# Moving one of two second-level minima to GpSimd, and the softmax statistics to one number per row, in a two-stage attention kernel

## The chip, the cores and the metric

The kernel runs on one core of one Trainium2 chip. The metric is the device time of one execution in microseconds (us); before the change the median of three runs is 1190.12 us (1189.49 to 1190.14). The engines are called by the profile's names: PE (TensorE), DVE (VectorE), ACT (ScalarE), POOL (GpSimd) and SP (SyncE, which issues the DMAs).

## The reference

Two attentions in a row, for 8 batches of 576 rows, float32:

```python
# 1: top-32 attention, 8 heads of width 64
scores = scale * np.matmul(q, k.transpose(0, 1, 3, 2))
kth = np.partition(scores, -32, axis=-1)[..., -32:-31]
scores = np.where(scores >= kth, scores, -1e9)
attn = softmax(scores)
x = np.matmul(attn, v)              # heads joined: 576 x 512 per batch
# 2: four experts (w_gate, wq, wk, wv, wo); the two with the larger logit count per row
logits = x @ w_gate
for e in range(4):
    a = softmax(causal(scale * (x @ wq[e]) @ (x @ wk[e]).T))
    out += weight_of(e) * (a @ (x @ wv[e]) @ wo[e])
```

## The kernel before, in words

**Tiling.** Two heads make a pair; there are 32 pairs, four to a batch. The 2 x 576 rows of a pair are nine tiles of 128 rows, in three groups of three tiles, so there are 96 groups in all. After every four pairs stands the second attention of that batch.

**One group (function `topk`).** PE multiplies the three tiles' scores, ACT copies them to `s` (L569). DVE then finds the 32 largest of each row of 576. It first folds the row: `f1` (L580) takes the larger of the halves into `fa`, `f3` (L583) the smaller into `fb`. `f4` folds `fa` once more: maxima of its halves into `cand` (L588), minima in place (L589), then from the maxima those of the next fold into `oct` (L591) and the minima beside them (L592). From there DVE works with MAX8 (eight largest of a row) and MATCH_REPLACE8 (strike eight values out): `f6` takes eight candidates from `fb` (L600), `f5` eight from each half of the minima in `fa` (L604, L605), and four rounds `win`/`rep` (L613, L618) take 8 of the 32 winners each, two from `oct` and two from `cand`.

POOL does small things for a group: `mark` (L596) copies one number of `oct` and so keeps what is queued behind it on POOL from starting earlier; `tails` (L608) copies the last candidates, and `compare` (L640), with a sign count on ACT, checks for the group before whether the candidates were enough. If the counts of the whole run say that they were not, a branch at L1249 runs a second, general pass over everything.

**Statistics (function `stats`, twice a pair).** For four or five tiles: differences to the row's maximum (`s1`, DVE, L700), exponentials (`s3`, ACT, L711), their sum (`s4`, DVE, L715), and logarithms. Maximum and logarithm go, each as a high and a low part, into four columns (`s2` on POOL, L706 and L707; `s6` on ACT, L725 and L726; `s7` on DVE, L730). PE transposes the four columns (`s8`, L734), ACT copies the rows into rows 64 to 67 of an operand (`s9`, L738), where the second product of the scores subtracts them.

**What sets the order.** Every step is a task with an engine, an assumed duration, a priority and buffers. `Plan.order` runs through them once with a table of priorities (`BIAS` and the `D_` numbers) and writes each engine's list of instructions; on the chip every engine follows its list in order. The list `PORT` names the DVE steps which the planner keeps apart from POOL's.

Of the kernel before, what the change touches and what calls it, by code (L numbers as in the profile page):

```python
# [10 lines left out]
FT = mybir.dt.float32  # L11
FR = mybir.dt.float32r
# [5 lines left out]
S = 576  # L18
D = 64
# [90 lines left out]
class Plan:  # L110
# [7 lines left out]
    PORT = ("f1", "f3", "f4", "s1", "s7", "ot", "constants", "sub", "low_again")  # L118
    SLACK = 100.9508
# [128 lines left out]
def pool(n):  # L248
# [7 lines left out]
BIAS = {"<lambda>": 432.2674, "again": 348.8874, "av": 0.3356, "avm": 369.6519, "c1": 80.5249, "c2": -8.8455, "c3":  # L256
        -45.1992, "c4": 1.7827, "c5": -12.4639, "cast": 189.9301, "cast_swap": 110.1952, "check1": 92.3392,
        "check2": 35.5895, "check3": -40.5142, "compare": -4.4354, "constants": -65.862, "copy": -161.6975, "count":
        229.2168, "diag": 42.7475, "dup": -188.6936, "dup1": -274.8919, "dup2": 295.4185, "e_stage": -264.9382,
# [3 lines left out]
        "g8": 176.5188, "g9": 85.871, "load_": -423.7509, "load_swap": -59.609, "loadv": 180.8196, "low_again":  # L263
        -141.4595, "m_stage": -469.5208, "mark": -298.151, "mask": 246.2406, "neg": 44.6072, "neg2": -127.4992,
# [3 lines left out]
        462.5432, "sub": 64.4327, "t_stage": 0.5767, "tails": 22.1925, "vproj": -19.8822, "win": 41.2933, "xh":  # L268
        154.0901, "xl": -80.96}
D_K2 = 84.27756  # L270
D_PREP = 21.53669
D_SC = 6.67649
D_TIE = -56.65601
D_MASK = -141.78759
D_STAT = -135.15358
D_TAIL = 0.07265
D_STEP = 0.10387
D_MOE = 4.215
D_LAST = 43.62471
D_PEN = 3.08857  # L280
D_SPAN = 3.51429
# [5 lines left out]
def kernel(ctx, tc, qk, vL, wq, wk, wv, wo, out):  # L287
# [42 lines left out]
    OCT = ring("oct", [P, 3, 72], FT, 2)  # L330
# [4 lines left out]
    STAT = sets("stat", 2, ([P, 5, TOPK], FT), ([P, 2, 5], FT), ([P, 5, 4], FR))  # L335
# [18 lines left out]
    def blank2(eng, x):  # L354
        t = K2[x].tiles[0]
        eng.memset(ft(t[0:64, gap(x)]), 0.0)
        eng.memset(ft(t[64:128, :]), 0.0)
        eng.memset(ft(t[64:68, OFF[x]:OFF[x] + S]), -8.0)
        eng.memset(ft(t[64:66, OFF[x]:OFF[x] + S]), -1.0)
# [11 lines left out]
    identf = sb.tile([P, P], FT, name="identf")  # L371
    identb = sb.tile([P, P], BF, name="identb")
# [177 lines left out]
    def topk(w, general):  # L550
# [4 lines left out]
        for g in range(3):  # L555
            js = (3 * g, 3 * g + 1, 3 * g + 2)
            s3, fa, fb, c = Buf(S3), Buf(FA), Buf(FB), Buf(CAND)
            oc = None if general else Buf(OCT)
# [26 lines left out]
            def f4(fa=fa, c=c, oc=oc):  # L585
# [37 lines left out]
            t = add("DVE", 1870, f4, [t], bufs=[fa, c, oc], prio=P0)  # L623
# [61 lines left out]
    def stats(w, x):  # L685
# [618 lines left out]
```

## Time and profile before

| what | before |
|---|---|
| median of 3 runs | 1190.12 us |
| the profiled execution's own time | 1187.17 us |
| its span, first to last instruction | 1185.4 us |
| busy PE / DVE / ACT / POOL | 1100.7 / 1090.6 / 982.9 / 377.2 us |
| granted TensorE clock, mean | 0.977 of full speed |

The profile is of one execution. Its span is the time between its first and last instruction; the execution's own time is 1.8 us longer. Busy time is time in which an instruction of the engine is recorded as running; instructions of one engine overlap a little, and starts are the safer measure: the time from the start of one instruction to that of the next is called a step here.

### The profile page before, as it was taken

Reading aid. Unit: us, or ns where it says so; the run is one execution under the profiler, and the core shown is the slowest. Engines: PE = TensorE matmul, PEld = TensorE weight load, DVE = VectorE, ACT = ScalarE, POOL = GpSimd, SP = SyncE. Lnnn points to the kernel's source line nnn. Section 1 sums busy time; section 2 is a strip of 40 time slices with the busy share of each in tenths; the row PEclk is TensorE's granted clock in tenths of the full one; section 3 lists DMA queues with packets and bytes.
Section 4 is the critical chain, followed back from the end, with each engine's and each line's share of the span. In section 5 each row is a group of like instructions: output and inputs, shape, how many; then the busy total and the mean of one; then the engine's idle time right before and its main releaser. Section 6 shows DMA issues by size and latency. Waiting matters only on the chain. (4 is left out here: it accounts for less than half of the span.)

```text
span 1185.4 us, 28265 instructions
## 1 busy us (share of the span) xinstructions
PE 1100.7 (93%) x9330; PEld 914.8 (77%) x9330; DVE 1090.6 (92%) x4745; ACT 982.9 (83%) x2050; POOL 377.2 (32%) x803
## 2 busy tenths in 40 slices
PE   3487799999999999999999999999999999999996
PEld 2366577787888878888888888888887878888785
DVE  7999999999999999999999999999999999999021
ACT  5677777989889997999889998899879997899554
POOL 4322222334323332243323333323332342322212
PEclk8689999999999999999999999999999999999999
DMA  7133332223432233333422233323432334320101
GB/s 204 44 92 87 83 91 64 77 63 100 123 92 68 72 105 84 82 91 94 116 82 69 64 99 111 92 67 93 118 82 61 83 101 118 93 51 21 39 6 44
DMA packets 45579, 98.56 MB, mean 83 GB/s; under 512 B 7792, under 2 KB 7792, under 8 KB 45424
## 3 DMA queue, kind: packets, MB, share of 16 engines
q1 hardware_dynamic: 45424, 96.67, 30.1%
q8 instruction: 76, 1.25, 0.4%
q14 instruction: 79, 0.65, 0.2%
HBM read 32.06 MB, written 9.44 MB: 35 GB/s over the span
## 5 line engine op out<-in xcount | busy, mean ns | idle before, releaser
L821 ACT ACTIVATE pt<-slot 128x576 f32<-128x576 f32 x288 | 186.3, 655 | 68.9 <-PE slot L302 66.8
L596 POOL COPY scrap<-oct 128x1 f32<-128x1 f32 x96 | 38.0, 396 | 590.2 <-DVE oct L591 585.0
L660 ACT ACTIVATE mask<-s,top 128x576 bf16<-128x576 f32 x288 | 215.4, 776 | 10.6 <-DVE top L613 10.2
L302 PE MATMUL slot<-opa,opa 128*128 128x256 f32 (+3 forms) x984 | 193.2, 321 | 20.9 <-ACT s L569 12.3
L302 PE MATMUL acc<-pt,vt 128*64 128x320 f32 (+3 forms) x1152 | 203.5, 421 | 3.2 <-ACT pt L821 2.5
L302 PE MATMUL slot<-opb,opb 128*128 128x320 f32 (+1 forms) x960 | 173.8, 306 | 4.8 <-ACT s L569 2.2
L569 ACT ACTIVATE s<-slot 128x576 f32<-128x576 f32 x288 | 174.1, 651 | 1.4 <-PE slot L302 1.0
L302 PEld LDWEIGHTS slot<-opa,opa 128*128 128x128 f32 (+1 forms) x984 | 145.8, 195 | 29.4 <-ACT s L569 13.2
L613 DVE MAX8 top<-cand 128x8 f32<-128x168 f32 x576 | 152.2, 319 | 0.0
L302 PEld LDWEIGHTS slot<-opb,opb 128*128 128x128 f32 x960 | 141.4, 191 | 11.8 <-ACT s L569 3.4
L302 PEld LDWEIGHTS acc<-pt,vt 128*64 128x64 f32 (+1 forms) x1152 | 95.4, 143 | 58.2 <-issue 20.4
L302 PEld LDWEIGHTS <-mask 128*128 128x128 bf16 (+1 forms) x1632 | 80.1, 101 | 61.3 <-issue 45.8
L302 PE MATMUL slot<-negi,mask 128*128 128x128 bf16 (+3 forms) x1632 | 125.4, 217 | 0.0
L600 DVE MAX8 cand<-fb 128x8 f32<-128x288 f32 x288 | 112.4, 446 | 0.0
L580 DVE TENSOR_TENSOR fa<-s 128x864 f32<-128x864 f32 x96 | 102.5, 1068 | 2.4 <-ACT s L569 2.4
L583 DVE TENSOR_TENSOR fb<-s 128x864 f32<-128x864 f32 x96 | 100.8, 1050 | 0.0
L640 POOL TENSOR_TENSOR ind<-cand,top 128x513 bf16<-128x513 f32 x96 | 100.5, 1047 | 0.5
L613 DVE MAX8 top<-oct 128x8 f32<-128x72 f32 x576 | 94.3, 218 | 0.0
L618 DVE MATCH_REPLACE8 cand<-top,cand 128x168 f32<-128x168 f32 x288 | 88.7, 318 | 0.0
L734 PE MATMUL slot<-identf,stat 128*4 128x128 f32 x288 | 43.5, 279 | 43.0 <-DVE stat L730 22.0
L648 ACT ACTIVATE ind<-ind,tiny 128x513 bf16<-128x513 bf16 (+1 forms) x96 | 70.7, 736 | 2.9 <-POOL ind L640 2.9
L302 PE MATMUL slot<-opa,k2a 128*128 128x256 f32 (+1 forms) x320 | 69.7, 300 | 1.2 <-ACT opa L738 1.2
(192 smaller groups left out, 2458.5 us busy)
## 6 DMA issues: line engine op xcount, KB each, us to landing
raw<-in_qk_dram SPq DMA_DIRECT2D x31, 576.0 KB, 3.7
opa<-raw SPq DMA_DIRECT2D x93, 144.0 KB, 2.4
opb<-raw SPq DMA_DIRECT2D x93, 144.0 KB, 3.3
vt<-in_vL_dram SPq DMA_DIRECT2D x32, 320.0 KB, 3.4
opa<-opa SPq DMA_DIRECT2D x62, 144.0 KB, 2.4
opb<-opb SPq DMA_DIRECT2D x62, 144.0 KB, 2.6
out_dram<-pr SPq DMA_DIRECT2D x32, 256.0 KB, 2.0
k2a<-opa SPq DMA_DIRECT2D x32, 144.0 KB, 2.3
```

Source lines behind the costliest of these rows:

```text
L302: nc.tensor.matmul(o, l, r, start=start, stop=stop, skip_group_check=True)
L569: nc.scalar.activation(s3.t[:, n], sl.t[:, o0:o0 + S], AF.Copy)
L580: v.tensor_tensor(out=fa.t, in0=s3.t[:, :, 0:288], in1=s3.t[:, :, 288:576], op=OP.max)
L583: v.tensor_tensor(out=fb.t, in0=s3.t[:, :, 0:288], in1=s3.t[:, :, 288:576], op=OP.min)
L600: v.max(out=c.t[:, n, 160:168], in_=fb.t[:, n])
L613: v.max(out=w.top.t[0][:, j, 8 * r:8 * r + 8], in_=oc.t[:, n] if r < 2 else c.t[:, n, 0:168])
L618: v.match_replace(out=c.t[:, n, 0:72] if r == 1 else src, in_values=src, imm_value=LOW, in_to_replace=w.top.t[0][:, j, 8 * r:8 * r + 8])
L640: nc.gpsimd.tensor_tensor(out=ind.t[:, 0:513].rearrange("p (a n) -> p a n", a=3), in0=c.t, in1=m32[:, js[0]:js[0] + 3, 31:32].to_broadcast ...
L648: nc.scalar.activation(ind.t[:, 0:n], ind.t[:, 0:n], AF.Sign, bias=tiny, accum_out=signs[:, 3 * w.p + g:3 * w.p + g + 1])
L660: nc.scalar.activation(w.mask[j].t, s3.t[:, n], AF.Relu, bias=w.top.t[0][:, j, 31:32], scale=-1.0)
L734: nc.tensor.transpose(sl.t[0:4, j * P:(j + 1) * P], ft(parts()[2][:, j]), identf)
L821: es[j] = add("ACT", act(S), lambda sl=sl, pt=pt, o0=o0: nc.scalar.activation(pt.t, sl.t[:, o0:o0 + S], AF.Exp, scale=0.125), [a], bufs=[s ...
```

## The change

- The minima at the second fold (L589) leave DVE. On POOL a new step `lesser` adds the bit patterns of the two halves as 32-bit integers, and subtracts that of the maximum, which leaves that of the minimum. The maxima go to a buffer of their own (`fc`), from which DVE makes `oct` and the minima of the third fold.
- `mark` now copies the last number of the last fold's output and stands, like `lesser` behind it, after DVE's last fold. `f5`, which needs the minima, moves on DVE from before the first two rounds to behind them and waits for `lesser`.
- The statistics are one number per row, an eighth of the maximum plus the logarithm, in a high and a low part: two columns for four. `s7` becomes three POOL instructions, `s2` one for two, `s6` one logarithm for two; `s8` multiplies by an identity in fp32r instead of transposing in fp32; two rows are added into the operand for four.
- The causal mask takes its factor from the other operand of the same products; one constant (`identb`) goes.
- All numbers of the planner's table are new, and so is the order.

```diff
-    PORT = ("f1", "f3", "f4", "s1", "s7", "ot", "constants", "sub", "low_again")
-    SLACK = 100.9508
+    PORT = ("f1", "f3", "f4", "s1", "ot", "constants", "sub", "low_again", "g1")
+    SLACK = 187.642
...
-    OCT = ring("oct", [P, 3, 72], FT, 2)
+    FC = ring("fc", [P, 3, 144], FT, 1)
+    OCT = ring("oct", [P, 3, 72], FT, 1)
...
-                l, r = fa.t[:, :, 0:144], fa.t[:, :, 144:288]
-                v.tensor_tensor(out=c.t[:, :, 0:144], in0=l, in1=r, op=OP.max)
-                v.tensor_tensor(out=l, in0=l, in1=r, op=OP.min)
-                l, r = c.t[:, :, 0:72], c.t[:, :, 72:144]
+                v.tensor_tensor(out=fc.t, in0=fa.t[:, :, 0:144], in1=fa.t[:, :, 144:288], op=OP.max)
+                l, r = fc.t[:, :, 0:72], fc.t[:, :, 72:144]
                 v.tensor_tensor(out=oc.t, in0=l, in1=r, op=OP.max)
-                v.tensor_tensor(out=r, in0=l, in1=r, op=OP.min)
+                v.tensor_tensor(out=c.t[:, :, 72:144], in0=l, in1=r, op=OP.min)
...
+            def lesser(fa=fa, fc=fc):
+                l, r, m = [x.bitcast(I32) for x in (fa.t[:, :, 0:144], fa.t[:, :, 144:288], fc.t)]
+                nc.gpsimd.tensor_tensor(out=l, in0=l, in1=r, op=OP.add)
+                nc.gpsimd.tensor_tensor(out=l, in0=l, in1=m, op=OP.subtract)
...
-                nc.gpsimd.tensor_copy(scrap[:, g:g + 1], oc.t[:, 0, 0:1])
+                nc.gpsimd.tensor_copy(scrap[:, g:g + 1], c.t[:, 2, 143:144])
...
-            marks.append(add("POOL", 200, mark, [t], bufs=[oc], prio=-9))
+            marks.append(add("POOL", 300, mark, [t], bufs=[c], prio=-9))
+            less = marks[-1] = add("POOL", 2300, lesser, [t, marks[-1]], bufs=[fa, fc], prio=-8)
             t = add("DVE", 3 * dve(288), f6, [t], bufs=[fb, c], prio=P0)
-            t = add("DVE", 6 * dve(72) - 45, f5, [t], bufs=[fa, c], prio=P0)
-            tl = add("POOL", 200, tails, [t], bufs=[c], prio=0)
             for r in range(4):
+                if r == 2:
+                    t = add("DVE", 6 * dve(72) - 45, f5, [t, less], bufs=[fa, c], prio=P0)
+                    tl = add("POOL", 200, tails, [t], bufs=[c], prio=0)
...
         def s6():
-            nc.scalar.activation(hl[:, :, 2], z[:, 0], AF.Ln, bias=eps)
-            nc.scalar.activation(z[:, 1], z[:, 0], AF.Ln, bias=eps)
+            nc.scalar.activation(z[:, 0], z[:, 0], AF.Ln, bias=eps)
         def s7():
-            nc.vector.tensor_tensor(out=hl[:, :, 3], in0=z[:, 1], in1=ft(hl[:, :, 2]), op=OP.subtract)
+            g.tensor_tensor(out=z[:, 1], in0=z[:, 0], in1=z[:, 2], op=OP.add)
+            g.tensor_copy(hl[:, :, 0], z[:, 1])
+            g.tensor_tensor(out=hl[:, :, 1], in0=z[:, 1], in1=ft(hl[:, :, 0]), op=OP.subtract)
         def s8():
-                nc.tensor.transpose(sl.t[0:4, j * P:(j + 1) * P], ft(parts()[2][:, j]), identf)
+                mm(sl.t[0:2, j * P:(j + 1) * P], parts()[2][:, j], identr, start=(j % 4 == 0))
```

DVE's list for one group of the second pair, before (names as above, with the buffer's number; `x3` is one for each tile):

```order
L580 TENSOR_TENSOR fa_89<-s_88 128x864
L583 TENSOR_TENSOR fb_90<-s_88 128x864
L588 TENSOR_TENSOR cand_94<-fa_89 128x3x144
L589 TENSOR_TENSOR fa_89<-fa_89 128x3x144
L591 TENSOR_TENSOR oct_92<-cand_94 128x216
L592 TENSOR_TENSOR cand_94<-cand_94 128x3x72
L715 TENSOR_REDUCE stat_1_115<-stat_0_114 128x5
L600 MAX cand_94<-fb_90 128x8 x3
L604 MAX cand_94<-fa_89 128x8
L605 MAX cand_94<-fa_89 128x8
```

The same place on DVE with the change:

```order
L581 TENSOR_TENSOR fa_89<-s_88 128x864
L584 TENSOR_TENSOR fb_90<-s_88 128x864
L588 TENSOR_TENSOR fc_91<-fa_89 128x432
L590 TENSOR_TENSOR oct_92<-fc_91 128x216
L591 TENSOR_TENSOR cand_94<-fc_91 128x3x72
L719 TENSOR_REDUCE stat_1_115<-stat_0_114 128x5
L605 MAX cand_94<-fb_90 128x8 x3
L618 MAX top_0_98<-oct_92 128x8 x3
L623 MATCH_REPLACE oct_92<-top_0_98,oct_92 128x72 x3
...
L623 MATCH_REPLACE cand_94<-top_0_98,oct_92 128x72 x3
L609 MAX cand_94<-fa_89 128x8
L610 MAX cand_94<-fa_89 128x8
```

One of five two-input instructions is gone, and the MAX instructions on `fa` have moved from behind `f6` to behind the first two rounds.

POOL's list from one `mark` to the next, third pair, before (`ind` is the check's scratch, `raw` the loaded inputs of the next pair but one, `x` the first attention's output):

```order
L596 COPY scrap<-oct_91 128x1
L706 CAST stat_2_116<-top_0_96 128x5
L707 TENSOR_TENSOR stat_2_116<-top_0_96,stat_2_116 128x5
L640 TENSOR_TENSOR ind_95<-cand_94,top_0_96 128x513
L482 TENSOR_TENSOR raw_68<-raw_68,opb_2_83 128x576
L841 CAST x_0_125<-x_0_125 128x64
L841 CAST x_1_126<-x_1_126 128x64
L608 COPY cand_93<-cand_93 128x3x3
```

And with the change:

```order
L601 COPY scrap<-cand_93 128x1
L596 TENSOR_TENSOR fa_89<-fa_89 128x3x144
L597 TENSOR_TENSOR fa_89<-fa_89,fc_91 128x3x144
L711 TENSOR_SCALAR stat_1_115<-top_0_96 128x5
L734 TENSOR_TENSOR stat_1_115<-stat_1_115 128x5
L735 CAST stat_2_116<-stat_1_115 128x5
L736 TENSOR_TENSOR stat_2_116<-stat_1_115,stat_2_116 128x5
L647 TENSOR_TENSOR ind_95<-cand_94,top_0_96 128x513
L613 COPY cand_93<-cand_93 128x3x3
L483 TENSOR_TENSOR raw_68<-raw_68,opb_2_83 128x576
```

Two instructions of 432 elements stand behind `mark`, four small ones of the statistics follow them, and the rest of the group's work comes after those.

## Rows read from the trace of the kernel before

**Rows 1.** The page's first part: busy us (share of the span) xinstructions.
```profile
PE 1100.7 (93%) x9330; PEld 914.8 (77%) x9330; DVE 1090.6 (92%) x4745; ACT 982.9 (83%) x2050; POOL 377.2 (32%) x803
```

**Rows 2.** Busy us by stretch: PE, PEld, DVE, ACT, POOL; then clock, DMA.
```profile
13.00:140.00 127.00, 87.11 (x601) 66.84 (x600) 125.80 (x563) 90.26 (x172) 41.03 (x70) 0.83 0.34 89
140.00:1097.00 957.00, 931.81 (x8054) 780.15 (x8055) 944.09 (x4122) 839.99 (x1770) 313.32 (x671) 1.00 0.32 85
1097.00:1186.00 89.00, 77.34 (x667) 64.04 (x663) 13.97 (x31) 44.71 (x100) 16.44 (x41) 0.97 0.09 29
```

**Rows 3.** Waits of DVE: who for whom, us in total, times, longest us.
```profile
DVE v L907 <- ACT v L904: 28.0, 13, 19.7
```

**Rows 4.** Groups of instructions by shape, DVE and ACT: busy us, mean ns, idle before.
```profile
L580 DVE TENSOR_TENSOR fa<-s 128x864 f32<-128x864 f32 x96 | 102.5, 1068 | 2.4 <-ACT s L569 2.4
...
L589 DVE TENSOR_TENSOR fa<-fa 128x432 f32<-128x432 f32 x96 | 58.4, 608 | 3.3
...
L726 ACT ACTIVATE stat<-stat,eps 128x5 f32<-128x5 f32 x32 | 9.3, 290 | 0.0
...
L730 DVE TENSOR_TENSOR stat<-stat,stat 128x5 fp32r<-128x5 f32 x32 | 5.3, 167 | 0.0
```

**Rows 5.** Timeline of DVE through one group: start us, duration us, instruction.
```profile
606.86 0.61 DVE L588 TENSOR_TENSOR cand<-fa 128x432 f32<-128x432 f32 x1
607.50 0.61 DVE L589 TENSOR_TENSOR fa<-fa 128x432 f32<-128x432 f32 x1
608.02 0.38 DVE L591 TENSOR_TENSOR oct<-cand 128x216 f32<-128x216 f32 x1
608.43 0.38 DVE L592 TENSOR_TENSOR cand<-cand 128x216 f32<-128x216 f32 x1
608.74 0.32 DVE L715 TENSOR_REDUCE stat<-stat 128x5 f32<-128x160 f32 x1
608.97 1.17 DVE L600 MAX8 cand<-fb 128x8 f32<-128x288 f32 x3
610.05 0.22 DVE L604 MAX8 cand<-fa 128x8 f32<-128x72 f32 x1
...
610.95 0.46 DVE L613 MAX8 top<-oct 128x8 f32<-128x72 f32 x3
...
612.94 0.16 DVE L730 TENSOR_TENSOR stat<-stat,stat 128x5 fp32r<-128x5 f32 x1
613.01 0.80 DVE L613 MAX8 top<-cand 128x8 f32<-128x168 f32 x3
...
615.45 0.29 DVE L700 TENSOR_TENSOR stat<-top 128x128 f32<-128x128 f32 x1
```

**Rows 6.** Groups of instructions by shape, POOL.
```profile
L640 POOL TENSOR_TENSOR ind<-cand,top 128x513 bf16<-128x513 f32 x96 | 100.5, 1047 | 0.5
...
L482 POOL TENSOR_TENSOR raw<-raw,opb 128x576 f32<-128x576 f32 x31 | 44.2, 1426 | 9.6 <-ACT opb L473 9.2
...
L596 POOL COPY scrap<-oct 128x1 f32<-128x1 f32 x96 | 38.0, 396 | 590.2 <-DVE oct L591 585.0 <-ACT pr L1071 5.2
...
L608 POOL COPY cand<-cand 128x9 f32<-128x9 f32 x96 | 18.9, 197 | 49.6 <-DVE cand L605 30.3 <-DVE stat L730 18.8
...
L428 POOL TENSOR_TENSOR wv<-ot,wv 128x1040 fp32r<-128x1040 f32 x1 | 2.4, 2413 | 5.6 <-ACT wv L426 5.6
```

**Rows 7.** Timeline of POOL and DVE where a long POOL instruction meets `f1`.
```profile
22.80 2.36 POOL L428 TENSOR_TENSOR wq<-ot,wq 128x1024 fp32r<-128x1024 f32 x1 [2.15 <-ACT wq L426]
...
23.90 2.18 DVE L580 TENSOR_TENSOR fa<-s 128x864 f32<-128x864 f32 x1
```

**Rows 8.** Timeline of PE: a statistics transpose, and eight matmuls of one step, twice.
```profile
613.58 0.71 PE L734 MATMUL slot<-identf,stat 128*4 128x128 f32 x5
...
630.03 1.19 PE L302 MATMUL acc<-pt,vt 128*64 128x256 f32 x8
...
696.09 1.95 PE L302 MATMUL acc<-pt,vt 128*64 128x256 f32 x8
```

More of the change, by code (lines that the diff above doesn't have):

```diff
@@ L11 @@
 FT = mybir.dt.float32
+I32 = mybir.dt.int32
 FR = mybir.dt.float32r
@@ L254 @@
 STAY = 0.0
[L256 to L259, printed above, removed]
[3 rows of a table removed]
-        "g8": 176.5188, "g9": 85.871, "load_": -423.7509, "load_swap": -59.609, "loadv": 180.8196, "low_again":
-        -141.4595, "m_stage": -469.5208, "mark": -298.151, "mask": 246.2406, "neg": 44.6072, "neg2": -127.4992,
[3 rows of a table removed]
[L268 to L281, printed above, removed]
+BIAS = {"<lambda>": 790.3207, "again": 544.1485, "av": -29.6551, "avm": 732.6632, "c1": -29.5585, "c2": -82.7498,
+        "c3": -85.8288, "c4": 182.7614, "c5": -40.7874, "cast": 203.739, "cast_swap": 259.5016, "check1": 366.5358,
+        "check2": 91.8723, "check3": 9.0544, "compare": -51.9199, "constants": 69.4778, "copy": -159.6793, "count":
[4 rows of a table added]
+        328.4265, "g9": 549.9019, "lesser": -2000.0, "load_": -51.5251, "load_swap": 55.3503, "loadv": 83.8137,
+        "low_again": -167.8865, "m_stage": -1173.3421, "mark": -2000.0, "mask": -116.1191, "neg": 226.036, "neg2":
[3 rows of a table added]
+        -317.2232, "store": -68.001, "sub": 332.0482, "t_stage": -4.4048, "tails": 12.0296, "vproj": -11.1804,
+        "win": 584.4638, "xh": -430.4561, "xl": 113.0599}
+D_K2 = 161.06314
+D_PREP = -12.70192
+D_SC = 76.95509
+D_TIE = -23.44819
+D_MASK = 182.29961
+D_STAT = -170.69951
+D_TAIL = -117.3015
+D_STEP = 28.78064
+D_MOE = 23.86418
+D_LAST = 146.51473
+D_PEN = 72.02683
+D_SPAN = 24.44548
 MP = (14,3)
@@ L357, in blank2 @@
         eng.memset(ft(t[64:128, :]), 0.0)
[L358 to L359 removed]
+        eng.memset(ft(t[64:66, OFF[x]:OFF[x] + S]), -8.0)
     def blank_later():
@@ L370 @@
     blank_later()
-    identf = sb.tile([P, P], FT, name="identf")
-    identb = sb.tile([P, P], BF, name="identb")
+    identr = sb.tile([P, P], FR, name="identr")
+    identf = ft(identr)
     negi = sb.tile([P, P], BF, name="negi")
@@ L388, in constants @@
         v = nc.vector
-        for t, op, f in ((identf, OP.is_equal, 1.0), (identb, OP.is_equal, 1.0), (negi, OP.is_equal, NEG),
-                         (tri, OP.is_gt, NEG), (negr, OP.is_equal, -1.0)):
+        for t, op, f in ((identr, OP.is_equal, 1.0), (negi, OP.is_equal, NEG),
+                         (tri, OP.is_gt, 1.0), (negr, OP.is_equal, -1.0)):
             v.tensor_scalar(t, jp, 0.0, f, op0=op, op1=OP.mult)
@@ L557, in topk @@
             s3, fa, fb, c = Buf(S3), Buf(FA), Buf(FB), Buf(CAND)
-            oc = None if general else Buf(OCT)
+            oc, fc = (None, None) if general else (Buf(OCT), Buf(FC))
             cps = []
@@ L622, in topk @@
             t = add("DVE", dve(864), f3, cps + [t], bufs=[s3, fb], prio=P0)
-            t = add("DVE", 1870, f4, [t], bufs=[fa, c, oc], prio=P0)
-            marks.append(add("POOL", 200, mark, [t], bufs=[oc], prio=-9))
+            t = add("DVE", 1370, f4, [t], bufs=[fa, fc, c, oc], prio=P0)
+            marks.append(add("POOL", 300, mark, [t], bufs=[c], prio=-9))
+            less = marks[-1] = add("POOL", 2300, lesser, [t, marks[-1]], bufs=[fa, fc], prio=-8)
             compare_last()
             t = add("DVE", 3 * dve(288), f6, [t], bufs=[fb, c], prio=P0)
-            t = add("DVE", 6 * dve(72) - 45, f5, [t], bufs=[fa, c], prio=P0)
-            tl = add("POOL", 200, tails, [t], bufs=[c], prio=0)
             for r in range(4):
                 n = 72 if r < 2 else 168
+                if r == 2:
+                    t = add("DVE", 6 * dve(72) - 45, f5, [t, less], bufs=[fa, c], prio=P0)
+                    tl = add("POOL", 200, tails, [t], bufs=[c], prio=0)
                 t = add("DVE", 3 * dve(n) - (25 if r < 2 else 0), lambda r=r, win=win: win(r), [t], bufs=[oc, c, w.top], prio=P0, tag="win")
@@ L703, in s2 @@
         def s2():
-            hl, mx = parts()[2], w.top.t[0][:, js, 0]
-            g.tensor_copy(hl[:, :, 0], mx)
-            g.tensor_tensor(out=hl[:, :, 1], in0=mx, in1=ft(hl[:, :, 0]), op=OP.subtract)
+            g.tensor_scalar(parts()[1][:, 2], w.top.t[0][:, js, 0], 0.125, None, op0=OP.mult)
         def s3():
@@ L742, in stats @@
         t = add("DVE", dve(32 * n), s1, top + ([] if w.general else made), bufs=b1, prio=0)
-        t2 = add("POOL", 480, s2, [t], bufs=b1, prio=0)
+        t2 = add("POOL", 160, s2, [t], bufs=b1, prio=0)
         t = add("ACT", act(32 * n, False), s3, [t], bufs=[st], prio=0)
@@ L747, in stats @@
             t = add("POOL", 400, s5, [t], bufs=b1, prio=0)
-        t6 = add("ACT", 375, s6, [t], bufs=[st], prio=0)
-        t7 = add("DVE", 75, s7, [t6], bufs=b1, prio=0)
-        t8 = add("PE", 443 if n == 4 else 545, s8, [t2, t7], bufs=[st, sl], prio=0, kind="TT")
+        t6 = add("ACT", 187, s6, [t], bufs=[st], prio=0)
+        t7 = add("POOL", 480, s7, [t2, t6], bufs=[st], prio=0)
+        t8 = add("PE", 245 if n == 4 else 300, s8, [t7], bufs=[st, sl], prio=0, kind="MM")
         return add("ACT", 767 if x == 0 else 610, s9, [t8],
@@ L1041, in causal @@
                             for h in range(2):
-                                mm(sl.t[:, 512 * h + t * P:512 * h + w], identb, tri, start=first)
+                                mm(sl.t[:, 512 * h + t * P:512 * h + w], negi, tri, start=first)
                         def prods(first):
```

14 lines of the change are left out of this document (7 added, 7 removed), and 13 rows, old and new, of the table BIAS.

## The prediction

> **What bounds the kernel now.** I read the page's first part, then busy time by stretch, then DVE's waits, then DVE's groups and one group's timeline, and last POOL's. The first part names two candidates, PE with 93% and DVE with 92% of the span [rows 1]. The stretches tell more [rows 2]. From 13 to 1097 us, in which all 96 groups run, DVE is busy 125.8 + 944.1 of 1084 us, and its waits are almost all behind that: of 28.0 us on L904 one wait alone is 19.7, and `f1`, which opens every group, waited for its input 2.4 us in all [rows 3, 4]. So DVE runs its list there without a hole, and 89 us follow in which PE finishes the last pair and the last batch (77.3 us busy) and DVE has 14 us of work [rows 2]. PE looks full too: 931.8 of 957 us. But its records overlap, so that a short wait between two matmuls leaves no idle time. The same eight matmuls of `av` took 1.19 us once and 1.95 us another time [rows 8]. A PE that is only just kept fed by DVE would show exactly this. I take DVE as the bound up to 1097 us, and PE as close behind.
>
> **The fold on DVE.** Before, the two-input run of a group's second and third fold lasts from 606.86 to the next instruction at 608.74: 1.88 us, in steps of 0.64, 0.52, 0.41 and 0.31 [rows 5]. L589 with its 96 instructions goes [rows 4]. The first of the three that stay keeps 0.64, since the next needs its result as now. The second is followed by one that does not read its output, so its step lies between 0.31 (L592, whose successor needs nothing of it) and 0.41 (L591, whose successor works in the same buffer). The third keeps 0.31. That makes 1.26 to 1.36 us and saves 0.52 to 0.62 a group; I take 0.62, as L592 is the nearer case: 96 x 0.62 = 59.5 us (50 at the other end). L730 goes as well: its step is 0.07 (612.94 to 613.01) [rows 5], 64 times (32 of each shape) [rows 4]: 4.5 us. Together DVE loses 64 us (54 at least).
>
> **The new wait.** DVE now reaches `f5` after `f6` (608.97 to 610.05, 1.08 us) and two rounds (610.95 to 612.94, 1.99 us): 3.07 us after the folds, and 0.23 more where L715 stands between [rows 5]. In that time POOL must do `mark` and two instructions of 432 elements. `mark` took 396 ns because it ran into L592; the like copy of `tails`, which meets nothing, takes 197 [rows 6]. No row shows an integer add on POOL. Of two-input work the rows give 1426 ns for 576 elements and 2413 for 1040, so 2.13 ns an element, and 1120 for 432; from below 882 (L640's 1047 for 513, in proportion), from above the 1426 of the longer instruction [rows 6]. I take 1.12 each, from the two with full operands. With 0.2 for `mark` and some 0.15 for handing over that is 2.6 us, so `f5` does not wait; at 1.43 each it is 3.2, and DVE waits 0.15 in groups without L715 in front, some 5 us in all; at 0.88 there is a microsecond to spare. Everything behind the waiting `f5` on DVE, and so the winners, the masks and the second products on PE, would wait with it.
>
> The trace puts the price of this work at 0.52 us on DVE against 2.24 on POOL. The Trainium skill, "GPSIMD Engine Reference", section "Engine selection", advises against elementwise work there, as about twice as slow for two inputs; the rows agree on the direction. By that page's 2.6 cycles an element (section "Elementwise"), an estimate of 0.94 us each would leave the sum as it is, with more to spare. The rule weighs the instruction and not the list that it delays.
>
> **POOL's list and the shared port.** POOL's busy time becomes 377 [rows 1] - 96 x 0.2 (`mark`) + 96 x 2.24 + 64 x 0.4 (four small statistics instructions of about 0.2, as L608 [rows 6], for two) = 602 us, 6.3 us a group. All of it is to fit between DVE's two-input runs, which is 608.81 to 615.45, 6.6 us [rows 5]: a long POOL instruction and a two-input DVE instruction do not run beside each other. At 22.80 POOL starts one of 2.36 us, and `f1`, begun at 23.90, takes 2.18 instead of its mean of 1.07 [rows 4]; its end at 26.08 is 0.92 after POOL's [rows 7]. The Trainium skill says the same of it, "SBUF — State Buffer", section "SBUF: two separate sides": the port pair of the two is locked for a whole instruction and the loser blocks fully. By that rule MAX8 with its one input would pay nothing. Before, POOL always had room: 585 us of waiting at `mark`, 6 us a group [rows 6]. Now POOL is some 95% full in that window, and some groups will run over, those of the second attention above all, where POOL gets a multiplication of 512 elements or a subtraction of 576 in addition. A group that runs over costs DVE about 1.2 us: up to 1.43 (L482's length [rows 6]), as a held `f1` or as a late `lesser`. Below nothing it cannot cost; above, it is one such piece for each of the 96 groups, 115 us. I take 12 groups, one or two a batch: 14 us.
>
> **PE, ACT, and the rest.** The statistics transposes are 288, five of them in 0.71 us, whose last one shows its own latency, so about 0.11 a step [rows 8]. No row has this product in fp32r; it saves between nothing and 0.11, I take half, 16 us, off DVE's path before 1097. ACT drops 64 logarithms of 290 ns [rows 4], minus overlap about 12 us of an engine with 840 of 957 busy [rows 2]. Both give room to engines that must now follow a faster DVE. The statistics' small parts on POOL stand behind `lesser`, which ends about when L730 ran before, 4 us behind L715. The new order can move a few us in the first batch and in the last 89 us; I put it at nothing, give or take 5. SP issues the same transfers, in a slightly other order.
>
> **The sum.** 1187.2 (the execution's own time) - 64 + 14 = 1137. The median of the runs is 3 us above the profiled execution, so 1140 us. Without any overrun it is 1126.
>
> **Rivals.** *PE becomes the bound.* For it: 931.8 of 957 us busy. If the records tell the truth, at most the 25 us of idle time, 14 of the statistics' 16 and 7 of the first batch (12 groups x 0.62) can go: 1144 in the median; if its idle time stays, 1169. In between, 1156. Against it: 1.19 and 1.95 us for the same matmuls [rows 8].
> *POOL comes too late, slower than before.* Besides its work, POOL waits in its list for ACT and DVE; `tails` alone waits 49.6 us [rows 6], and since it stands behind `f5`, POOL may not start what follows early. If every group runs over, 115 - 64 = +51 us: 1241. The change loses from the 54th group of 96 on (64 / 1.2). This is the lock at work, the page's rule taken to its end; against it speaks that light groups have only `mark`, `lesser`, `compare` and `tails`, 3.7 us. Half way, 30 to 50 groups, the time is 1162 to 1186.
> *The integer minima are not exact.* Then the counts fail and the second pass runs: at least DVE's 1090 us [rows 1] again, over 2200.
>
> **How the numbers follow.** DVE stays the bound and some groups overrun: 0.52, 1130 to 1152. No overrun, and the order gains a little: 0.12, 1120 to 1130. PE (or ACT) takes over: 0.18, 1145 to 1169. POOL late in 30 to 50 groups: 0.10, up to 1186. In more: 0.07, slower, 1190 to 1241. Second pass: 0.01. Less than 0.2% (2.4 us) cannot be told from no change. Faster is 0.52 + 0.12 + 0.18 + 0.09 = 0.91, the same 0.01, slower 0.08. The range 1122 to 1172 leaves out the late POOL and a sliver at the fast end, and takes in 54 instead of 64 and the 5 us either way.
>
> **What would show it.** DVE's folds from the first to the instruction behind them in 1.26 us, and its busy time down by 60 or more. `f5` without a wait for `lesser`. `f1` at its mean of 1.07, or else with a tail of long ones. The end of DVE's groups near 1047 instead of 1097, with the 89 us behind it as they are. The integer instructions at 1.12 us. I am wrong if DVE's idle time between the groups grows to 20 us or more and ends with PE or ACT, or with POOL at `f5`.

## The result, and the profile after

The change makes the kernel faster, by much less than forecast: 1173.38 us (median of four runs, 1172.02 to 1173.81) beside 1190.13 on the same chip, a ratio of 0.986 (95% interval 0.9844 to 0.9875). That is 16.8 us where 50 were expected, and the time lies just above the range.

The page's first part (busy us, share of the span, instructions) and the three stretches (PE, PEld, DVE, ACT, POOL, then clock and DMA) answer to [rows 1, 2]; the span is now 1172.0 us.

```profile
PE 1098.9 (94%) x9330; PEld 909.8 (78%) x9330; DVE 1047.6 (89%) x4584; ACT 977.5 (83%) x1986; POOL 591.0 (50%) x1121
```
```profile
13.00:140.00 127.00, 87.92 (x597) 67.29 (x597) 125.82 (x548) 90.91 (x167) 68.41 (x108) 0.80 0.34 89
140.00:1097.00 957.00, 940.39 (x8178) 782.99 (x8178) 902.75 (x3982) 842.49 (x1727) 506.25 (x963) 1.00 0.32 86
1097.00:1186.00 89.00, 65.11 (x537) 54.67 (x536) 11.95 (x25) 35.47 (x81) 11.15 (x30) 0.97 0.07 26
```

DVE has 43.0 us less to do (1090.6 to 1047.6), but its idle time, span minus busy, has grown from 94.8 to 124.4 us. So 29.6 of the 43.0 us came back as waiting, and the span is 13.4 us shorter. The waits of DVE (who for whom: us, times, longest), beside [rows 3, 4], where `f1` waited 2.4 us in all. First three with the change, then two of before:

```profile
DVE fa L581 <- ACT s L570: 17.7, 20, 2.1
DVE fa L1068 <- PE slot L303: 13.8, 4, 7.2
DVE stat L719 <- ACT stat L715: 8.2, 13, 1.4
```
```profile
DVE fa L1062 <- PE slot L302: 13.4, 4, 6.8
DVE stat L715 <- ACT stat L711: 0.4, 1, 0.4
```

Two waits make up most of what is new: `f1` (now L581) waits for ACT's copy of the scores 20 times, 15.3 us more than before, and the sum of the statistics (L719) for ACT's exponentials 13 times, 7.8 us more. The wait at L1068 was there before.

One batch (four pairs, 12 groups) is read from the first `f1` of two batches that follow each other (shortest, median and longest duration in ns, then first and last start in us). Before:

```profile
L580 DVE TENSOR_TENSOR fa<-s x1: 1046/1046/1046, 549.6 to 549.6; 128x864 f32<-128x864 f32 x1
...
L580 DVE TENSOR_TENSOR fa<-s x1: 1051/1051/1051, 686.4 to 686.4; 128x864 f32<-128x864 f32 x1
```

and with the change:

```profile
L581 DVE TENSOR_TENSOR fa<-s x1: 1059/1059/1059, 541.2 to 541.2; 128x864 f32<-128x864 f32 x1
...
L581 DVE TENSOR_TENSOR fa<-s x1: 1058/1058/1058, 676.2 to 676.2; 128x864 f32<-128x864 f32 x1
```

This batch went from 136.8 to 135.0 us, though the folds in it take 12 x 0.65 = 7.8 us less of DVE (the steps below). All 96 `f1`, before and after:

```profile
L580 DVE TENSOR_TENSOR fa<-s x96: 1037/1050/2176, 13.2 to 1083.7; 128x864 f32<-128x864 f32 x96
```
```profile
L581 DVE TENSOR_TENSOR fa<-s x96: 1036/1052/2644, 12.6 to 1068.0; 128x864 f32<-128x864 f32 x96
```

The last group begins 15.7 us earlier, where the forecast had DVE's groups end 50 us earlier.

The fold itself does what was forecast. Of the six two-input instructions of a group on DVE five are left. DVE and POOL through one group (start, duration, instruction), beside [rows 5]:

```profile
601.73 1.42 POOL L483 TENSOR_TENSOR raw<-raw,opb 128x576 f32<-128x576 f32 x1
...
602.25 1.05 DVE L707 TENSOR_TENSOR stat<-top 128x128 f32<-128x128 f32 x1
603.23 1.05 DVE L581 TENSOR_TENSOR fa<-s 128x864 f32<-128x864 f32 x1
...
605.16 0.59 DVE L588 TENSOR_TENSOR fc<-fa 128x432 f32<-128x432 f32 x1
605.79 0.38 DVE L590 TENSOR_TENSOR oct<-fc 128x216 f32<-128x216 f32 x1
606.09 0.38 DVE L591 TENSOR_TENSOR cand<-fc 128x216 f32<-128x216 f32 x1
606.39 0.28 DVE L719 TENSOR_REDUCE stat<-stat 128x4 f32<-128x128 f32 x1
...
606.67 1.12 POOL L596 TENSOR_TENSOR fa<-fa 128x432 int32<-128x432 int32 x1
...
607.87 1.12 POOL L597 TENSOR_TENSOR fa<-fa,fc 128x432 int32<-128x432 int32 x1
...
609.69 0.23 DVE L609 MAX8 cand<-fa 128x8 f32<-128x72 f32 x1
```

From 605.16 to 606.39 the folds take 1.23 us (1.88 before), and each integer instruction 1.12. The first rows also show the price on the shared port: `s1` (L707), which took 0.29 in [rows 5], takes 1.05 beside POOL's subtraction.

### The profile page after: what moved, and what is told of

It is laid out like the page before. It is cut to its first block, busy times and chain, and to the rows that moved or that the text cites. A ratio compares the mean times of both kernels' runs of the same rounds, so it can differ in the third digit from the quotient of the medians.

```text
span 1172.0 us, 28335 instructions
## 1 busy us (share of the span) xinstructions
PE 1098.9 (94%) x9330; PEld 909.8 (78%) x9330; DVE 1047.6 (89%) x4584; ACT 977.5 (83%) x1986; POOL 591.0 (50%) x1121
## 5 line engine op out<-in xcount | busy, mean ns | idle before, releaser
L601 POOL COPY scrap<-cand 128x1 f32<-128x1 f32 x96 | 18.1, 189 | 401.5 <-DVE cand L591 390.5
L667 ACT ACTIVATE mask<-s,top 128x576 bf16<-128x576 f32 x288 | 211.4, 772 | 2.8 <-DVE top L618 2.4
L303 PE MATMUL acc<-pt,vt 128*64 128x256 f32 (+3 forms) x1152 | 202.8, 425 | 2.1 <-ACT pt L827 2.0
L303 PE MATMUL slot<-opb,opb 128*128 128x320 f32 (+1 forms) x960 | 179.8, 309 | 7.0 <-DMA opb<-raw 6.0
L581 DVE TENSOR_TENSOR fa<-s 128x864 f32<-128x864 f32 x96 | 112.7, 1174 | 17.7 <-ACT s L570 17.7
L597 POOL TENSOR_TENSOR fa<-fa,fc 128x432 int32<-128x432 int32 x96 | 106.7, 1111 | 7.5
L596 POOL TENSOR_TENSOR fa<-fa 128x432 int32<-128x432 int32 x96 | 107.0, 1114 | 0.0
L303 PE MATMUL slot<-opb,k2b 128*128 128x320 f32 x320 | 69.7, 300 | 2.0 <-ACT opb L744 2.0
```

The lines of the kernel that those rows point to most:

```text
L303: nc.tensor.matmul(o, l, r, start=start, stop=stop, skip_group_check=True)
L581: v.tensor_tensor(out=fa.t, in0=s3.t[:, :, 0:288], in1=s3.t[:, :, 288:576], op=OP.max)
L596: nc.gpsimd.tensor_tensor(out=l, in0=l, in1=r, op=OP.add)
L597: nc.gpsimd.tensor_tensor(out=l, in0=l, in1=m, op=OP.subtract)
L667: nc.scalar.activation(w.mask[j].t, s3.t[:, n], AF.Relu, bias=w.top.t[0][:, j, 31:32], scale=-1.0)
```

## Experiments

All were timed in at least three rounds beside the kernel before, on several chips. Since that kernel's median moves with the chip (1188.7 to 1192.5 us), the ratios to it are compared; 1% is 11.9 us, and a difference of two ratios is uncertain by some 0.2%. "After" is the changed kernel, at 0.986. In all of them every engine's list keeps its order; only the named instructions differ. Where an edit touches the candidates or their count (e3 to e7, e9, e10, e12, e15, e18), the limit that starts the second pass is out of reach as well.

| run | kernel and edit | us | ratio (95%) |
|---|---|---|---|
| e1 | after, PE cut | 1157.9 | 0.9719 (0.9703 to 0.9735) |
| e2 | before, PE cut | 1171.9 | 0.9843 (0.9826 to 0.9859) |
| e3 | after, POOL cut | 1170.8 | 0.9826 (0.9809 to 0.9842) |
| e4 | after, DVE cut | 1173.8 | 0.9848 (0.9817 to 0.9879) |
| e5 | after, PE and DVE cut | 1150.9 | 0.9659 (0.9643 to 0.9675) |
| e6 | after, ACT cut | 1170.2 | 0.9815 (0.9798 to 0.9832) |
| e7 | after, PE and POOL cut | 1154.0 | 0.9684 (0.9668 to 0.9701) |
| e8 | after, minima on DVE again | 1197.0 | 1.0048 (1.0032 to 1.0065) |
| e9 | after, all four cuts | 1133.1 | 0.9501 (0.9485 to 0.9518) |
| e10 | after, PE and ACT cut | 1153.2 | 0.9671 (0.9655 to 0.9687) |
| e11 | after, PE work added | 1231.1 | 1.0324 (1.0306 to 1.0341) |
| e12 | before, DVE cut | 1187.8 | 0.9966 (0.9947 to 0.9984) |
| e13 | after, old transposes | 1179.1 | 0.9924 (0.9906 to 0.9941) |
| e14 | before, new transposes | 1190.2 | 1.0013 (0.9995 to 1.0030) |
| e15 | before, PE and DVE cut | 1167.9 | 0.9807 (0.9790 to 0.9823) |
| e16 | after, no wait at `s8` | 1171.8 | 0.9858 (0.9842 to 0.9875) |
| e17 | before, no wait at `s8` | 1188.6 | 1.0005 (0.9992 to 1.0018) |
| e18 | before, both savings | 1185.1 | 0.9943 (0.9924 to 0.9961) |

### One engine relieved at a time, after the change (e1, e3, e4, e6)

```diff
 # e1, PE: third product of the second attention's projections (q and k; likewise v and o)
-for i, (w, x) in enumerate(((WT[name][0], xh), (WT[name][0], xl), (WT[name][1], xh))):
+for i, (w, x) in enumerate(((WT[name][0], xh), (WT[name][0], xl))):
 # e3, POOL: lesser is empty
-nc.gpsimd.tensor_tensor(out=l, in0=l, in1=r, op=OP.add)
-nc.gpsimd.tensor_tensor(out=l, in0=l, in1=m, op=OP.subtract)
 # e4, DVE: f6 on half its row
-v.max(out=c.t[:, n, 160:168], in_=fb.t[:, n])
+v.max(out=c.t[:, n, 160:168], in_=fb.t[:, n, 0:144])
 # e6, ACT: the sign count
-nc.scalar.activation(ind.t[:, 0:n], ind.t[:, 0:n], AF.Sign, bias=tiny, ...
+nc.scalar.activation(ind.t[:, 0:8], ind.t[:, 0:8], AF.Sign, bias=tiny, ...
```

> The changed kernel in its own order, with less work on PE alone: of the three products of high and low parts the last one is left out in the second attention's v, q, k and output projections (20, 32 and 10 matmuls a batch, some 8.9 us a batch by their steps of 0.118, 0.131 and 0.230 us, about 70 us in all). Theory A (PE sets the pace in the steady part, its busy records tell the truth): the time falls by 25 us or more, until DVE takes over, to 1120 to 1148. Theory B (DVE sets the pace, held up by POOL at the shared port and at f5): PE's work is beside DVE's, the time falls by the last batch's part alone, about 9 us, to 1160 to 1168.

> The changed kernel in its own order without the two integer instructions on POOL (f5 then reads maxima of the first fold instead of the minima; the second pass is never taken): 215 us less on POOL, the same on DVE. Theory A: POOL is beside the path, within 6 us of the changed kernel's 1173. Theory B: the collisions and the lateness go, the time falls by 20 us or more, to 1153 or less.

> The changed kernel in its own order with less work on DVE alone: f6 looks at 144 of 288 numbers (three times 0.15 us a group, 43 us in all; the second pass is never taken). Theory A: DVE is not the bound, the time falls by less than 8 us. Theory B: it falls by 30 us or more, to 1143 or less.

> The changed kernel in its own order with less work on ACT alone: the sign count looks at 8 instead of 513 numbers (about 0.5 us a group, some 48 us in all; the second pass is never taken). Theory C: within 5 us of 1173. Theory D with ACT as the bound: it falls by 20 us or more, to 1153 or less.

Measured against "after": PE -1.4%, which is 17 us where 70 were planned and PE's busy time falls by 57 (page below); POOL -0.3%; ACT -0.5%; DVE no difference that can be told, with 38 us less busy time. None gives back what was taken from it. e3, e4 and e6 are the first case of their expectations; e1 falls between its two theories. `f1` tells where e1 gains: 6.9 us before the last group begins (1068.0 to 1061.1), though some 61 us of PE work go in the first seven batches, and the rest, 8.7 us of the profiled spans, behind it.

```profile
PE 1041.4 (90%) x8834; PEld 843.9 (73%) x8834; DVE 1047.7 (91%) x4584; ACT 974.9 (84%) x1986; POOL 589.7 (51%) x1121
```
```profile
L581 DVE TENSOR_TENSOR fa<-s x96: 1036/1053/2659, 12.5 to 1061.1; 128x864 f32<-128x864 f32 x96
```

Without POOL's integer work the kernel is about 4 us faster, so neither `lesser` nor the port it holds explains the 33 us that are missing.

### The same cut of PE before the change (e2)

> The same PE work left out of the kernel before. Both theories: there DVE ran without a hole, so only the last batch's part, behind DVE's groups, can go: 1178 to 1185. If it falls by 25 us or more, PE was the bound before the change already and DVE's gapless list followed it.

It gives 1.6%, about what e1 gives after, and falls between the two cases that were expected. PE was no freer before the change than behind it.

### Pairs, and all four (e5, e7, e10, e9)

The edits are those above, put together.

> The changed kernel in its own order with both cuts at once: the last product in the second attention's projections left out on PE (70 us of matmuls) and f6 on 144 of 288 numbers on DVE (43 us; the second pass is never taken). Theory C (PE and DVE are bound side by side, each lets the other's saving lie): the time falls well below the 1158 of the PE cut alone, by 25 us or more, to 1133 or less. Theory D (with PE relieved neither of them sets the pace, but ACT or the hand-overs between the lists, through three PSUM slots): within 8 us of 1158.

> The PE cut together with the integer instructions on POOL left out (f5 then reads maxima of the first fold; the second pass is never taken). If, with PE relieved, DVE is held by POOL (the shared port and the wait at f5), the time falls from 1158 by 12 us or more; if POOL is beside the path there too, it stays within 5 us of 1158.

> The changed kernel with PE and ACT relieved together (third product of the projections left out; sign count on 8 of 513 elements). Theory, the chain with hand-overs: the two gains add up, 15.5 + 3, so 1152 to 1156. Rival, ACT stands as a bound behind PE: the pair gives clearly more than its parts, 1145 or less (48 us of ACT are 6 a batch).

> The changed kernel with four engines relieved at once: PE (third product of the second attention's v, q, k and o projections left out, about 70 us, 8.9 a batch), DVE (f6 on 144 of 288 elements, 43 us), ACT (sign count on 8 of 513 elements, about 48 us) and POOL (both integer instructions left out, 214 us). Theory, one chain that hands over from engine to engine by lists in a fixed order: every cut shortens only the pieces of the chain that lie on its engine, so that the gains of the single cuts about add up: 15.5 + 0 + 3 + 2.6 and the few us that the pairs gave beyond that, 1140 to 1150. Rival, engines as bounds close to one another, each hiding the others' cut: with all relieved the next bound lies at least 5.4 us a batch lower, 12 groups of 0.45 from f6, so 1173 - 43 - 8.5 for the last batch = 1122 or less.

Against "after": -2.0%, -1.8%, -1.9% and -3.6%. With PE relieved, the cut of DVE adds 0.6% (e5, within the 8 us of theory D), that of POOL 0.4% (e7, within 5 us) and that of ACT 0.5% (e10, the two gains added). The single gains add up to 1.4 + 0.1 + 0.5 + 0.3 = 2.3%, 28 us; all four together give 43. That is more than a chain whose pieces add, and less than bounds side by side (51 or more by the expectation): e9 fell between its two theories and decides for neither. Busy shares by its page:

```profile
PE 1044.5 (92%) x8834; PEld 849.6 (75%) x8834; DVE 1003.1 (88%) x4584; ACT 937.2 (83%) x1986; POOL 387.8 (34%) x929
```

With work taken from all four, their shares are almost those of "after" (94, 89, 83), POOL's apart. A share near 90% follows here from what the lists wait for, and does not say which engine sets the time.

### The minima back on DVE, new order (e8)

```diff
 def f4:
     v.tensor_tensor(out=c.t[:, :, 72:144], in0=l, in1=r, op=OP.min)
+    v.tensor_tensor(out=fa.t[:, :, 0:144], in0=fa.t[:, :, 0:144], in1=fa.t[:, :, 144:288], op=OP.min)
 def lesser: # empty
```

> The changed kernel in its own order with the minima made by DVE again, behind the folds, and nothing in their place on POOL: DVE gets 96 x 0.52 us = 50 us back. If DVE was the only bound before and is 50 us faster by the move, the time rises by 40 us or more, to 1213. If the moved work lies beside PE now, it rises by what DVE's own list then lacks against PE's 134.8 us a batch, under 20 us: 1176 to 1193.

1.9% (22 us) slower than "after", between the two expected cases, for 41 us more busy time of DVE (1088.3), and 0.5% slower than the kernel before. So without the moved minima nothing of the gain is left. They are not all of it either: e13 below loses half of the gain while the minima stay on POOL.

### PE work added (e11)

```diff
-for i, (w, x) in enumerate(((WT[name][0], xh), (WT[name][0], xl), (WT[name][1], xh))):
+for i, (w, x) in enumerate(((WT[name][0], xh), (WT[name][0], xh), (WT[name][0], xl), (WT[name][1], xh))):
```

> The changed kernel with the first product of the same projections issued twice (the second overwrites the first), so that PE gets about as much work more as the first experiment took away, 70 us, of it 61 in the first seven batches and 8.5 in the last. Theory, the chain passes through PE for a part of its way and PE's list has slack in the rest: clearly less than one for one, +20 to +45, 1193 to 1218. Rival, PE is the bound after the change and its records tell the truth: one for one but for its idle time of about 2.3 us a batch, +50 to +70, 1223 to 1243. Second rival, DVE is still the bound and PE only looks full: under +12 (the last batch alone), below 1185.

+4.6%, 55 us: the rival's case, PE one for one but for its idle time. Its page:

```profile
PE 1161.9 (95%) x9826; PEld 976.0 (79%) x9826; DVE 1049.8 (85%) x4584; ACT 980.6 (80%) x1986; POOL 598.9 (49%) x1121
```

With e1 this is a kink: 63 us more of PE work by the page (1098.9 to 1161.9) cost 55, and 57 less bring 17. After the change PE stands near the edge: work added to these steps counts almost in full, and when they get shorter something else decides.

### DVE relieved before the change (e12)

The edit of e4, in the kernel before.

> The kernel before with f6 on 144 of 288 elements: 43 us less on DVE, 5.4 a batch, with the order, POOL's work and everything else as they were. The prediction's theory, DVE is the bound of the kernel before until 64 us have gone: 1190 - 40, 1148 to 1155. Rival, something else stands close behind DVE already in the kernel before, as the 24 us suggest that the change gave for 64: 1165 to 1180. If it is above 1185, DVE was no bound at all, and the gain of the change comes from its new order.

-0.3%, 4 us for 43 planned: neither the prediction's theory nor the rival, but the last case, above 1185, in which DVE by itself is no bound before the change. `f6` before and here, 43.2 us apart, and the page of e12:

```profile
L600 DVE MAX8 cand<-fb 128x8 f32<-128x288 f32 x288 | 112.4, 446 | 0.0
```
```profile
L600 DVE MAX8 cand<-fb 128x8 f32<-128x144 f32 x288 | 69.2, 296 | 0.0
```
```profile
PE 1104.1 (93%) x9330; PEld 916.7 (77%) x9330; DVE 1062.7 (89%) x4745; ACT 982.3 (83%) x2050; POOL 387.6 (33%) x803
```

DVE is busy 27.9 us less than in [rows 1], and of a span of 1189.1 us it idles 126.4, 31.6 more than before; this execution took 3 us more than its run's median and that of [rows 1] 3 us less, so some of the 31.6 is scatter. The forecast's main premise falls here: in the kernel before DVE runs without a hole, and yet time taken from it comes back as waiting.

### The statistics' transposes, by themselves and their waits (e13, e14, e16, e17)

```diff
 # e13 (after)
-mm(sl.t[0:2, j * P:(j + 1) * P], parts()[2][:, j], identr, start=(j % 4 == 0))
+nc.tensor.transpose(sl.t[0:2, j * P:(j + 1) * P], ft(parts()[2][:, j]), identf)
 # e14 (before)
-nc.tensor.transpose(sl.t[0:4, j * P:(j + 1) * P], ft(parts()[2][:, j]), identf)
+mm(sl.t[0:4, j * P:(j + 1) * P], parts()[2][:, j], identr, start=(j % 4 == 0))
 ... # the identity is kept in fp32r for it
 # e16 (after), e17 (before, as a transpose of identf[:, 0:4]): a constant in place of the statistics
+mm(sl.t[0:2, j * P:(j + 1) * P], identr[:, 0:2], identr, start=(j % 4 == 0))
```

> The changed kernel with s8 as before, 288 transposes in fp32 instead of matmuls in fp32r; all lists in the same order. It puts back about 15 us of PE work (43.5 - 28.6). New theory, PE's way through the batch sets the time and its shorter statistics are a large part of the gain: +9 to +15, 1182 to 1189. Rival, the gain came from DVE's shorter list: the 15 us lie in PE's waits, +0 to +4, 1173 to 1178.

> The kernel before with s8 in the new form (fp32r against the identity, still four columns), nothing else changed. New theory: -8 to -15, 1176 to 1183, since it takes 15 us from PE alone. Rival, DVE is the bound before: no change, 1188 to 1192.

> The changed kernel with s8 multiplying a constant instead of the statistics, so that PE waits for nothing there (27.2 us of idle time in front of it); what s9 copies is then not the statistics. If PE's waits for the statistics are on the way that sets the batch: -12 to -25, 1148 to 1161. If the wait only moves to the next slot or to the next operand: within 5 us, 1168 to 1178.

> The same in the kernel before, where 43.0 us of PE's idle time stand in front of the transposes (22.0 behind s7, 20.6 behind the winners on DVE). If these waits are on the way that sets the batch, and DVE is not: -20 to -40, 1150 to 1170. If DVE's list stands close behind, since it idles only some 2 us a batch: -5 to -15, 1175 to 1186. If the wait moves: within 3 us.

The transposes' groups of "after" and e13 (busy us, mean ns, idle before):

```profile
L303 PE MATMUL slot<-identr,stat 128*2 128x128 f32 x288 | 28.6, 228 | 27.2 <-POOL stat L736 26.0 <-ACT s L570 0.3
```
```profile
L740 PE MATMUL slot<-identr,stat 128*2 128x128 f32 x288 | 43.5, 280 | 30.2 <-POOL stat L736 28.2 <-ACT s L570 0.3
```

The same 15 us of these records are worth 0.6% (8 us) in the new order, between what the two theories gave, and nothing in the old one. PE's busy time as a whole differs by 4 us only (1098.9 and 1103.2 after, 1100.7 and 1096.3 before). So PE's way through the batch is not the explanation by itself either: e14 rules it out for the kernel before. The waits are worth nothing in either (e16, e17): the cases in which the wait moves. PE's waits in "after", first line, and in e16 show where they went:

```profile
PE slot L303 <- POOL stat L736: 26.0, 17, 14.3
```
```profile
PE slot L303 <- ACT s L570: 19.7, 6, 8.5
PE acc L303 <- ACT pt L827: 8.3, 9, 2.1
```

PE no longer waits for the statistics and waits for ACT, above all for its copy of the scores, instead.

### Both savings, and larger cuts together, in the old order (e18, e15)

```diff
 # e18 (before): L589 left out, and the products of e14
-v.tensor_tensor(out=l, in0=l, in1=r, op=OP.min)
 # e15 (before): the edits of e2 and e12
```

> The kernel before in its own order with the minima of L589 left out (58 us of DVE, no work on POOL in their place) and s8 in the new form (15 us of PE). If the two savings act together as those of two bounds side by side, the old order gives what the change gave, or more, since POOL has nothing to add: 1165 to 1176. If the lists of the old order pass the time saved on one engine to a wait on the next, and the gain of the change is one of its new order: 1182 to 1190.

> The kernel before with both cuts: third product of the second attention's projections left out (70 us of PE) and f6 on half its row (43 us of DVE). Alone they gave 18.6 and 4.7. PE and DVE as bounds side by side, each hiding the other's cut: clearly more than the sum, 1150 or less. One chain that hands over: about the sum, 1165 to 1170.

e18 gains 0.6% (7 us), though it has the two savings and POOL has nothing to do in return; the change gains 1.4%. That is the second case, savings that the old lists pass on to a wait. What the change has besides (the moved `f5`, other buffers, one logarithm for two, the new order) was not taken apart, so "new order" stands for all of that here. Its page, what DVE waits for, and two of these waits in the kernel before:

```profile
PE 1094.1 (92%) x9330; PEld 910.1 (77%) x9330; DVE 1054.2 (89%) x4649; ACT 982.8 (83%) x2050; POOL 389.2 (33%) x803
```
```profile
DVE v L907 <- ACT v L904: 35.4, 24, 19.7
...
DVE sm L1062 <- ACT x L837: 9.4, 6, 2.1
...
DVE ot L1162 <- PE slot L302: 7.2, 9, 1.2
```
```profile
DVE sm L1062 <- ACT x L837: 1.5, 2, 0.8
...
DVE ot L1162 <- PE slot L302: 0.3, 1, 0.3
```

DVE is busy 36.4 us less, and of the span of 1184.1 us idles 129.9, 35.1 more: nearly the whole saving has become idle time, and the waits that grew most (7.9, 7.4 and 6.9 us) stand at the second attention's steps, for ACT and for PE. e15 gives 1.9%, no more than e2 and e12 together (1.6 + 0.3): in the old order the two cuts only add, so PE and DVE are not two bounds that hide nothing but each other.

## Why the prediction was wrong, point by point

- *DVE as the bound: the step that failed.* "So DVE runs its list there without a hole" is what [rows 2 to 4] show, but for 14 us of idle time; "I take DVE as the bound up to 1097 us, and PE as close behind" does not follow. An engine without holes has no room for more work; that less work will save time is another claim, and e12 tests it: 43 us planned off DVE, 4 us gained. e18 tests the forecast's own saving: 58 us of L589 off DVE and the cheaper `s8`, 7 us gained. More work on DVE was run with the new order alone (e8: 41 us more busy time cost 22). The sum counted all 64 us of DVE's saving; about a quarter arrived. The Trainium skill ("Perfetto Trace Analysis", section "Identifying the Most-Contended Engine") calls the engine with the highest occupancy the most contended one, to be optimized first, and judges TensorE by other measures. DVE at 92% was that in [rows 1], and the measurement differs: relieving it gave 0.3%.
- *PE close behind.* The argument from [rows 8], 1.19 and 1.95 us for the same matmuls, was to show that PE's busy share hides stalls. It does (e1 takes 57 us of busy time and gains 17), but e11 shows that these steps have hardly any room after the change. The rival "PE becomes the bound" named 1144 to 1169, the last "if its idle time stays"; the time is 4 us behind that end. It is right only in one direction, as e1 and e11 show together. The rival "POOL comes too late" has the measured time in its 1162 to 1186, but not for its reason: `f5` does not wait for `lesser`, and without `lesser` (e3) 4 us go.
- *The folds*: 1.26 us a group forecast, 1.23 found. *The integer instructions*: 1.12 each, and 1.114 and 1.111 on average, in these groups of POOL:

```profile
L596 POOL TENSOR_TENSOR fa<-fa 128x432 int32<-128x432 int32 x96 | 107.0, 1114 | 0.0
L597 POOL TENSOR_TENSOR fa<-fa,fc 128x432 int32<-128x432 int32 x96 | 106.7, 1111 | 7.5
...
L601 POOL COPY scrap<-cand 128x1 f32<-128x1 f32 x96 | 18.1, 189 | 401.5 <-DVE cand L591 390.5 <-DVE v L913 11.0
```

- *The new wait.* Right: in the group above `lesser` ends at 608.99 and `f5` (L609) begins at 609.69, straight behind the round before it. `mark` still waits 401.5 us in all (590.2 in [rows 6]), so POOL has room, and takes 189 ns, as forecast, now that nothing runs beside it on two inputs; its busy time is 591.0, forecast 602 (the terms given there add up to 599).
- *The port.* 14 us forecast. In DVE's groups `f1` has 112.7 us (102.5 in [rows 4]) and `s1` (L707) 16.0 and 11.6. After:

```profile
L581 DVE TENSOR_TENSOR fa<-s 128x864 f32<-128x864 f32 x96 | 112.7, 1174 | 17.7 <-ACT s L570 17.7
...
L707 DVE TENSOR_TENSOR stat<-top 128x128 f32<-128x128 f32 x32 | 16.0, 501 | 1.1
...
L707 DVE TENSOR_TENSOR stat<-top 128x160 f32<-128x160 f32 x32 | 11.6, 363 | 0.0
```

  and before, `s1` alone:

```profile
L700 DVE TENSOR_TENSOR stat<-top 128x160 f32<-128x160 f32 x32 | 9.8, 308 | 0.0
L700 DVE TENSOR_TENSOR stat<-top 128x128 f32<-128x128 f32 x32 | 9.6, 300 | 0.9
```

  That is 18 us, near the forecast, as busy time of DVE, and by its size most of what keeps the saving at 43 instead of 64. The number came out partly by luck: the forecast had groups run over because of the two integer instructions, and without them (e3) 14 of the 18 us stay; `f1` there has

```profile
L581 DVE TENSOR_TENSOR fa<-s 128x864 f32<-128x864 f32 x96 | 109.9, 1145 | 18.3 <-ACT s L570 18.3
```

  In the rows shown it is the subtraction on `raw` (L483) that holds `s1` and `f1`; the new list has it behind `tails`, just before these two. But the port decides nothing: e4 takes more than that from DVE and gains nothing.
- *PE's statistics.* 16 us forecast, 43.5 to 28.6 found in these records, though 4 in PE's busy time (e13); "off DVE's path" was right for the old order (e14: nothing) and wrong for the new one (e13: 8 us).
- *The order.* "I put it at nothing, give or take 5." In the old order the savings give 0.6% (e18), in the new one without the minima moved there is a loss of 0.5% (e8), and both together give 1.4%. So the order is no term to be added to the saving: the two count only together. That it is the order that turns the saving into time is the reading that fits; the old order with every edit of the change was not run.
- *The sign of being wrong.* "I am wrong if DVE's idle time between the groups grows to 20 us or more and ends with PE or ACT": it grew by 29.6 us over the whole span, and `f1` alone waits 17.7 for ACT. DVE's busy time fell by 43, where 60 or more were the sign of being right.

What held the time instead can be followed in the traces: from the last `f1` back to the first `f1` of the second batch, at each step to what released an instruction or, if it had not waited, to the one before it on its engine. The us of this chain on each engine, and on the transfers of the next pairs' inputs (loads of `raw`, copies to `opa` and `opb`):

| run | in all | PE | DVE | ACT | POOL | transfers |
|---|---|---|---|---|---|---|
| before | 945 | 379 | 345 | 132 | 4 | 59 |
| e2, before, less PE | 937 | 63 | 820 | 17 | 4 | 7 |
| e12, before, less DVE | 952 | 540 | 64 | 187 | 3 | 131 |
| e18, before, both savings | 947 | 564 | 39 | 177 | 5 | 131 |
| after | 932 | 521 | 200 | 129 | 45 | 15 |
| e11, after, more PE | 979 | 789 | 45 | 110 | 24 | 0 |

Before the change the chain lies on PE and DVE in like parts. With less PE work it lies on DVE almost throughout, with less DVE work on PE, ACT and the transfers: several ways through a batch are about equally long there, and shortening one leaves the others. What a row lacks to its sum is time in which no wait is seen. The releasers are inferred, and of two ways of nearly equal length the chain takes one, so the parts are rough.

What stays open: how much each of these ways could give, and what the new order by itself is worth. No run shortens the transfers or ACT's part in the old order, or gives PE more slots or DVE more buffers; the runs show that no single engine and no wait at `s8` is the cause, and e9 shows that the pieces do not simply add.

## What to carry to other kernels

A busy share of 92% and no holes say that an engine has no room for more; whether it gives time if it gets less is another question, and halving one instruction on it in the kernel before (e12) answers it in one run. Where lists are written out in a fixed order, do not count a saving in full: in the old order about a tenth arrived (e18, 7 of 73 us planned), with an order made anew about a quarter, and the engine next in fullness (PE here, where added work costs nearly one for one in e11) may stand in the way of more. Test the supposed bound in both directions: e1 and e11 together say more than either.

## What the runs showed of the hardware

- An add or subtract of 432 32-bit integers in each of 128 partitions takes 1.11 us on POOL, what the rate of fp32 instructions in [rows 6] gave. MAX8 beside it is not slowed: `f6` takes 447 ns on average (446 before).
- A two-input DVE instruction that meets a POOL instruction on two inputs waits for its end, to within 0.15 us: above, `s1` takes 1.05 us for 0.29 and ends 0.15 behind POOL's subtraction, and here `f1`, which takes 1.05 alone, takes 1.79:

```profile
612.43 1.43 POOL L483 TENSOR_TENSOR raw<-raw,opa 128x576 f32<-128x576 f32 x1
612.98 1.79 DVE L581 TENSOR_TENSOR fa<-s 128x864 f32<-128x864 f32 x1
```

  The Trainium skill ("SBUF — State Buffer", section "SBUF: two separate sides") states this lock for the whole instruction, and the trace agrees: `f1`'s end, 614.77, is 0.91 us behind POOL's, most of its own 1.05.
- Turning the two statistics columns of 128 rows through a 128 x 128 identity takes 280 ns on average as a transpose in fp32 (e13) and 228 as a matmul in fp32r (after); 288 of them, in runs of four or five, have records of 43.5 and 28.6 us. Whether that is worth anything depends on the list around it: 8 us in one order, nothing in the other.
